# One of four transposing DMAs replaced by TensorE transposes, with a new hand-tuned task order

## The chip, the cores and the metric

The kernel runs on one core of one Trainium2 chip, as one launch. The metric is the device time of that launch in microseconds (us), lower is better. Each kernel was run several times. Names used below: PE is TensorE's matmul stream, DVE is VectorE, ACT is ScalarE, POOL is GpSimd, SP is the queue that issues hardware DMAs. "L512" is line 512 of the kernel's source.

## What is computed

Attention over 4 batches, 8 heads, 768 positions and 64 features per head. Heads 0, 2 and 6 see all earlier positions; heads 1, 3, 4, 5 and 7 see the last 64 positions and the first 4 ("sinks"). Its output, laid out as 3072 tokens by 512 features, goes through a gated feed-forward block. Shortened:

```python
scores = q @ k.T / 8, masked by head;  a = softmax(scores)
x = (a @ v) laid out as [3072, 512]
h = gelu(x @ w_gate) * (x @ w_val)              # 512 -> 1536
out = x + sigmoid(x @ w_res) * (h @ w_out)      # 1536 -> 512
```

## The kernel before

**Tiles and chunks.** The 3072 tokens are cut into six chunks of 512 tokens (`CHUNKS`; counted from 0, so the third chunk is chunk 2). Each chunk runs through the same stages. Attention comes first: for each of four head pairs, scores by TensorE into PSUM (L889, and L980 for the sinks), the exponential on ACT (L905), masks on DVE (L941), then the weighted sum of values on TensorE (L1013 for windows, and a helper at L512 and L513 for the rest), and the normalisation on DVE (L1078, L1080). Then come the matmuls with `w_gate` and `w_val` (called g and v, 96 per chunk and four per output block), gelu on ACT (L1162), and the product on DVE (L1164). Last come the outputs: `w_res` with a tanh (L1222), and seven products that make four output tiles of a pair from Strassen-like sums (L1253, L1277, L1282), and the write to memory from SP (L1288, and L1323 for the first pair of chunk 0).

**From tokens to features.** g and v need the normalised attention output with features on the partitions. The normalised values of a chunk are kept as 16-bit numbers in a buffer `x16` with two feature blocks of 128 at a time; two head pairs fill it, and it is then transposed into `xT`. Two ways stand in the source. `to_features` (L1100) makes four TensorE transposes of 128 by 128 per feature block (L1102) into a PSUM bank and one copy out of it by ACT or DVE (L1110). `to_features_dma` (L1092) makes one transposing DMA on SP (L1093) for both blocks. In chunks 0 and 1 all blocks go by TensorE. From chunk 2 (`DT_FIRST = 2`) the head pairs run in the order `LATER = (1, 3, 0, 2)`; the pairs 1 and 3, heads 4 to 7, fill feature blocks 2 and 3 first, and those go by DMA; blocks 0 and 1 follow by TensorE. The g and v matmuls over blocks 0 and 1 are tasks of their own and can run before blocks 2 and 3 are there.

**Loads.** POOL issues the loads that convert to 16 bits (L573). q and k of chunks 0 and 1 are transposed by TensorE (L705). From chunk 2 on SP issues eight transposing DMAs per chunk (L750) into `qkt`, and after a chunk's eight a copy of one head pair to other partitions, `q6` (L758); some of pair 1's score matmuls read `q6`. SP also issues the shifted copies of the values (L658). Each engine and each queue takes its instructions strictly in order.

**Who sets the order.** Every step is a task with an engine, an estimated cost, dependencies and a priority. A list scheduler written into the kernel (`Graph.schedule`) plays the tasks through with these estimates, and always starts the ready task of least priority number on each free engine; steps that two engines can do are given to the one that it expects to end first. The result is written out as fixed programs. Priorities follow a formula by chunk, and `HINTS` replaces single ones by numbers found beforehand; it lists them as task number and priority. Before the first g matmul the scheduler fills TensorE's idle time with matmuls on a blank tile (L1329). TensorE's instructions have four shapes: full 128 by 128, 64 rows (scores), 64 columns (windows, and from chunk 4 on nearly everything: L513 makes two 64-column matmuls of one) and 32 columns (sinks).

Of the kernel before, what the change touches and what calls it, by code (L numbers as in the profile page):

```python
# [39 lines left out]
DT_FIRST = 2  # L40
# [3 lines left out]


HINTS = (
    "1:-386.23 2:-51 9:-20.36 13:-200.31 428:1584.78 430:2007.77 436:2368.39 479:1475.25 482:1765.54 488:3518.86 "
    "537:6004.49 590:-192.92 609:-256.97 629:-1503.05 631:-966.95 638:-550.03 640:1715 643:232.16 648:262.35 "
    "656:219.8 674:810.58 675:-1134.51 703:38.07 711:336.34 712:-434.62 737:822.34 738:826.12 744:1130.99 "
    "750:1939.31 762:2550.75 767:1830.91 784:2410.9 787:-692.73 789:834.8 798:450.11 800:1192.39 805:3841.63 "  # L50
    "820:3905.53 831:1160.84 836:1677.33 837:940.96 841:627.82 848:508.5 865:-2323.53 877:2285.32 887:4400.62 "
    "898:3238.78 899:2548.8 906:2576.13 912:2498.5 918:2936.84 924:1499.5 955:3175.78 966:-173.61 967:2046.76 "
    "995:1370.62 1002:3719.58 1046:-2213.54 1051:2730.57 1053:3518.36 1060:4609.91 1063:5481.78 1087:3849.56 "
    "1119:6736.31 1120:3930.26 1131:2217.51 1137:3231.1 1138:3413.04 1143:2240.9 1150:3031.82 1156:5375.26 "
    "1168:2688.73 1187:2924.17 1196:2995.04 1216:2986.66 1243:1919.94 1247:2487.19 1252:5888.14 ~1253:3022.82 "
    "1257:2882.45 1260:4488.19 1309:6553.9 1315:4359.05 1326:4428.99 1367:1389.25 1372:1438.57 1374:3076.99 "
    "1387:1535.74 1388:5404.31 1391:3284.75 1451:6195.97 1454:3725.08 1457:4058.45 1459:6087.7 1478:5553.53 "
    "1481:6338.68 1482:6987.75 1495:6022.19 1510:6238.59 1511:4500.43 1513:5525.29 1520:4702.46 1525:4688.12 "
    "1530:4497.68 1538:4518.95 1544:4765.44 1547:2063.36 1549:4494.08 1562:6734.76 1567:1912.78 1568:5555.5 "
    "1577:4575.28 1591:4650.14 1594:5639.66 1596:9005.87 1614:9375.82 1619:4948.93 1622:4608.22 1654:6049.7 "  # L60
    "1659:4821.79 1673:5059.01 1674:6102.86 1678:6739.11 1688:4250.3 1689:6738.61 1691:14432.3 1744:5230.02 "
    "1800:10962.76 1802:6852.52 1803:7158.99 1804:6852.02 1805:7238.81 1811:7250.63 1817:6501.37 1818:5640.4 "
    "1820:10984.41 1835:7399.5 1836:6974.76 1839:7253.61 1840:7168.5 1842:7201.48 1843:7310.06 "
)

class Task:
# [42 lines left out]
class Pool:  # L109
# [7 lines left out]
    def can(self, kind, t):  # L117
        if kind in self.caps:
            h = self.held.get(kind, [])
            h[:] = [f for f in h if f is None or f > t]  # L120
            if len(h) >= self.caps[kind]:
                return False
        return any(f <= t for f, _ in self.free)
# [346 lines left out]
def build_kernel(nc, q, k, v, w_gate, w_val, w_out, w_res, out):  # L470
# [129 lines left out]
    def batch(b):  # L600
        if b not in batches:
            B_ = B()
            B_.v, B_.vs, B_.vk, B_.qkt = Buf(P_v), Buf(P_vs), Buf(P_vk), Buf(P_qkt)
            B_.vtok, B_.vstok, B_.qtok, B_.ktok = {}, {}, {}, {}

            B_.q6, B_.q6tok = None, {}
            batches[b] = B_
        return batches[b]
# [158 lines left out]
    def ph(c, part):  # L767
        return phase.setdefault((c, part), [])

    def attention(c, segs, xbuf, xtbuf, xtoks, xttoks, l0=0, last=(), ek=None, shared=None):  # L770
        tiles = [(b, i) for (b, a, z) in segs for i in range(a, z)]

        base = 1000 * c - (200 if len(tiles) < 4 and not l0 else 0)
        n0 = len(ph(c, "sc"))
        todo = []
        order = ORDER if c < DT_FIRST else LATER
        for k_, p in enumerate(order):
            P = B()
            P.heads, P.p, P.c, P.pr = PAIRS[p], p, c, base + 40 * k_
            retr = [IS_RETRIEVAL[h] for h in P.heads]  # L780


            banks, lower = [], []
            for x in range(2):
                mine = [[(b, i if retr[x] else None, i, 1) for b, i in tiles]]
                rest = [(b, kt, max(a, kt + 1), z - max(a, kt + 1)) for b, a, z in segs for kt in range(z - 1)] if retr[x] else []
                for r in sorted(rest, key=lambda r: -r[3]):
                    for bk in mine:
                        if sum(y[3] for y in bk) + r[3] <= 4:
                            bk.append(r)  # L790
                            break
                    else:
                        mine.append([r])
                if p == 1 and x == 1:

                    can = lambda bk: all((0, i) in batch(b).q6tok and (1, kt) in batch(b).q6tok
                                         for b, kt, q0, nq in bk for i in range(q0, q0 + nq))
                    left, mine = sorted(mine[1:], key=lambda bk: -sum(y[3] for y in bk)), mine[:1]
                    low = [bk for bk in left if can(bk)]
                    up = [bk for bk in left if not can(bk)]  # L800
                    while up or low:
                        mine.append((up or low).pop(0))
                        if low or up:
                            lower.append(id(low[0])) if low else None
                            mine.append((low or up).pop(0))
                banks += [(g, x, bk) for g, bk in enumerate(mine)]
            size = lambda t: sum(y[3] for y in t[2])
            if p != 1:
                banks.sort(key=lambda t: (t[0], -size(t), t[1]))
            else:  # L810
                banks.sort(key=lambda t: (t[0], -size(t) if not t[0] else 0, t[1]))
            P.et, P.off = (shared or {}).get(p, (None, 0))
            if P.et is None:
                P.et = Buf((P_eb if p else P_ea) if any(retr) else P_es)
            P.where, P.ready = {}, {}
            for g in range(0, len(banks), 2):
                scores(P, tiles, [t[1:] + (id(t[2]) in lower,) for t in banks[g:g + 2]], g, retr)
            if shared is not None and any(retr):
                shared[p] = P.et, P.off
            todo.append(P)  # L820
        sinks = sink_scores(c, [t for t in tiles if t[1] > 0], base + 40 + 5, ek, 256 if l0 else 0)
        for t in ph(c, "sc")[n0:-1]:
            if t.name[2:] in (str(order[2]), str(order[3])):
                t.order.append(ph(c, "sc")[-1])

        sc = ph(c, "sc")[:-1]
        for t, u in zip(sc[0::2], sc[1::2]) if c else ():
            t.deps += u.deps
            u.order.append(t)
            for b in u.bufs[:1]:  # L830
                t.bufs.append(b)
                b.left += 1
                b.users.append(t)
        norms = []
        for P in todo:
            if P.heads[0] % 2 == 0:
                x16 = Buf(P_x16)
                xdeps = []
            last, tn = weigh(P, tiles, sinks, xbuf, x16, xtoks, xdeps, last, l0)
            if P.heads[0] % 2 == 1:  # L840
                if c >= DT_FIRST and P.p == order[1]:
                    to_features_dma(c, P.heads[0] // 2, P.pr, x16, xdeps, xtbuf, xttoks)
                else:
                  for cb in (P.heads[0] // 2, P.heads[1] // 2):
                    to_features(c, cb, P.pr, x16, xdeps, xtbuf, xttoks, l0, len(tiles))
                if P is todo[-1]:
                    tn.order += [t for _, t in xttoks[-2:]]
                if c == 0 and P is todo[-1]:
                    for t in norms[1:]:
                        t.order.append(xdeps[-1])  # L850
            norms.append(tn)
        return last
# [239 lines left out]
    def to_features_dma(c, cb, pr, x16, xdeps, xtbuf, xttoks):  # L1092
        t = G.add("sp", 1.3, lambda e: e.dma_start(  # L1093
            at(xtbuf)[:, cb:cb + 2, :].rearrange("p c (i k) -> p (c i) k", k=128), at(x16)[:, :, :, :].rearrange("p c i k -> p (c i k)"), transpose=True),
            xdeps, pr - 4003, bufs=[x16, xtbuf], dma=1.2, name="xD")
        t.late = 2.5 if c == 2 else 1.0
        ph(c, "xT").append(t)
        xttoks += [(cb, t), (cb + 1, t)]
# [342 lines left out]
```

## Time and profile before

| | |
|---|---|
| median of 5 runs | 267.15 us (266.10, 266.24, 267.15, 268.81, 269.13) |
| profiled execution, its own time | 267.77 us |
| its span, first to last instruction | 266.0 us |
| granted TensorE clock | 1.00 |

Busy time in five stretches of the profiled execution, us:

| stretch | what runs | PE | DVE | ACT | POOL |
|---|---|---|---|---|---|
| 0 to 20 | loads, attention of chunk 0 | 16.00 of 20 | 10.32 | 10.29 | 17.20 |
| 45 to 67 | outputs of chunk 0, attention of chunk 1 | 22.00 of 22 | 19.05 | 15.84 | 8.65 |
| 67 to 88 | g and v of chunk 1 | 21.00 of 21 | 13.16 | 7.71 | 15.73 |
| 88 to 108 | outputs of chunk 1, attention of chunk 2 | 20.00 of 20 | 16.90 | 16.88 | 8.07 |
| 258 to 266 | last adds and writes | 3.73 of 8 | 5.35 | 0.60 | 2.29 |

An engine's busy time is what its instructions cover; PE's includes the blank matmuls. In the chain of waits, each piece is a start, a length, an engine and a line, with a count of instructions; a piece ends where the next thing that the end had to wait for begins. "To landing" is the time from a DMA's issue until its data has arrived.

### The profile page before, as it was taken

To read this page: it belongs to the slowest core of one execution; us is meant where nothing else is said; L and a number is where in the kernel's file an instruction comes from. 1 tells how busy PE (TensorE), PEld (TensorE's weight loads), DVE (VectorE), ACT (ScalarE), POOL (GpSimd) and SP (SyncE) were. 2 spreads that over 40 slices of the span, in tenths; PEclk is the share of its full clock that TensorE was granted. 3 is DMA by queue.
4 is the path that set the end of the run, shared out by engine and by line. 5 is a ranking of instruction groups with operands and counts; after the bars stand their busy time and mean duration, and the time that the engine had idled before them with its cause. 6 is when DMAs were issued, how large, how long until landed. Compare 5 with 4: busy or idle time off the path is not lost.

```text
span 266.0 us, 7506 instructions
## 1 busy us (share of the span) xinstructions
PE 257.4 (97%) x3234; PEld 166.6 (63%) x3234; DVE 181.8 (68%) x384; ACT 145.0 (55%) x229; POOL 89.7 (34%) x127
## 2 busy tenths in 40 slices
PE   7699999999999999999999999999999999999993
PEld 6567665457544577544477544679655589766792
DVE  2489536789656688664878645888448678936656
ACT  2576349875143889233786333787334887233430
POOL 8979979611995080994000000000000000000003
PEclk9999999999999999999999999999999999999999
DMA  6999999999999999999999300013110003110013
GB/s 83 160 205 206 187 175 229 176 152 170 129 152 237 172 130 144 190 157 184 183 154 147 126 0 0 2 43 84 39 43 0 2 2 82 58 65 0 2 38 123
DMA packets 97569, 29.49 MB, mean 111 GB/s; under 512 B 85504, under 2 KB 94080, under 8 KB 97536
## 3 DMA queue, kind: packets, MB, share of 16 engines
q0 software_dynamic: 70320, 14.69, 69.6%
q1 hardware_dynamic: 27216, 14.33, 29.9%
q8 instruction: 25, 0.41, 0.6%
q14 instruction: 8, 0.07, 0.1%
HBM read 29.36 MB, written 6.29 MB: 134 GB/s over the span
## 4 chain that ended last, share of the span: by engine, by line
PE 91%; DVE 4%; DMA 3%; POOL 1%; issue 0%; POOLq 0%
PE ps L512 48%; PE ps L513 32%; PE ps L889 5%; DMA qks<-in_k_dram 3%; PE ps L1013 2%; PE ps L1102 1%; PE ps L705 1%; DVE otile L1277 1%; POOL qks L573 1%; PE ps L1329 1%; PE ps L980 1%; DVE vs L642 1%; DVE otile L1253 1%; DVE otile L1282 0%; DVE x L1078 0%
## 5 line engine op out<-in xcount | busy, mean ns | idle before, releaser
L1162 ACT ACTIVATE gact<-ps 128x512 f16<-128x512 f32 x68 | 40.4, 597 | 72.5 <-PE ps L512 44.6
L1164 DVE SCALAR_TENSOR_TENSOR hT<-gact,ps 128x512 f16<-128x512 f16 x68 | 45.5, 686 | 46.9 <-ACT gact L1162 18.7
L512 PE MATMUL ps<-xT,wg 128*128 128x512 f16 (+1 forms) x208 | 50.6, 363 | 0.0
L512 PE MATMUL ps<-xT,wv 128*128 128x512 f16 (+1 forms) x202 | 50.2, 362 | 0.0
L1282 POOL TENSOR_TENSOR otile<-otile,xtok 128x256 f32<-128x256 f32 x3 | 2.3, 764 | 137.6 <-DVE otile L1277 137.6
L512 PEld LDWEIGHTS ps<-xT,wg 128*128 128x128 f16 x208 | 20.0, 98 | 20.9 <-DVE hT L1164 0.2
L573 POOL DMA_DIRECT2D qks<-in_k_dram x36 | 28.2, 815 | 13.1 <-DMA qkt<-qks 9.8
L512 PEld LDWEIGHTS ps<-xT,wv 128*128 128x128 f16 x202 | 19.4, 98 | 18.7 <-issue 0.3
L513 PE MATMUL ps<-xT,wv 128*64 128x512 f16 x204 | 29.4, 379 | 0.0
L573 POOL DMA_DIRECT2D qks<-in_q_dram x36 | 28.4, 828 | 2.4 <-issue 1.6
L573 POOL DMA_DIRECT2D va<-in_v_dram x24 | 21.3, 929 | 18.1 <-PE ps L512 18.1
L513 PE MATMUL ps<-xT,wg 128*64 128x512 f16 x192 | 27.2, 379 | 0.0
L905 ACT ACTIVATE ea<-ps 128x1024 f16<-128x1024 f32 (+2 forms) x24 | 21.1, 915 | 2.2 <-PE ps L889 1.9
L1253 DVE TENSOR_TENSOR otile<-otile,ps 128x256 f32<-128x256 f32 x33 | 13.6, 415 | 7.7 <-PE ps L512 3.1
L513 PEld LDWEIGHTS ps<-xT,wv 128*64 128x64 f16 x204 | 12.8, 110 | 8.9 <-ACT gact L1162 0.4
L1222 ACT ACTIVATE srs<-ps 128x512 f32<-128x512 f32 x22 | 13.1, 597 | 8.7 <-PE ps L513 5.9
L513 PEld LDWEIGHTS ps<-xT,wg 128*64 128x64 f16 x192 | 12.3, 110 | 7.9 <-DVE hT L1164 0.2
L1080 DVE TENSOR_TENSOR xtok<-ps,rcp 128x512 f32<-128x512 f32 (+1 forms) x28 | 16.7, 608 | 0.1
L889 PE MATMUL ps<-qkt 64*128 64x64 f16 (+4 forms) x391 | 16.3, 213 | 0.4 <-DVE xT L1110 0.4
L513 PE MATMUL ps<-wr,xT 128*64 128x512 f16 x120 | 15.3, 380 | 0.0
L889 PEld LDWEIGHTS ps<-qkt 64*128 64x128 f16 x391 | 9.7, 94 | 8.0 <-issue 4.0
L512 PE MATMUL ps<-wo,hT 128*128 128x256 f16 (+1 forms) x84 | 14.2, 303 | 0.0
(109 smaller groups left out, 437.1 us busy)
## 6 DMA issues: line engine op xcount, KB each, us to landing
out_dram<-otile SPq DMA_DIRECT2D x22, 256.0 KB, 3.2
va<-in_v_dram POOLq DMA_DIRECT2D x24, 128.0 KB, 13.4
qks<-in_k_dram POOLq DMA_DIRECT2D x32, 64.0 KB, 16.7
qks<-in_q_dram POOLq DMA_DIRECT2D x32, 64.0 KB, 16.5
wg<-in_moe_w_gate_dram POOLq DMA_DIRECT2D x3, 512.0 KB, 12.8
wv<-in_moe_w_val_dram POOLq DMA_DIRECT2D x3, 512.0 KB, 14.6
wo<-in_moe_w_out_dram POOLq DMA_DIRECT2D x4, 384.0 KB, 23.0
vs<-va SPq DMA_DIRECT2D x4, 260.0 KB, 8.4
```

The source lines that it names most:

```text
L512: return e.matmul(o, lhsT=lhsT, rhs=rhs, **k)
L513: return [e.matmul(o[h:h + 64], lhsT=lhsT[:, h:h + 64], rhs=rhs, **k) for h in (0, 64)][-1]
L573: return G.add(eng, issue, lambda e: e.dma_start(out_ap(), in_ap), deps, prio, bufs=bufs, dma=cost, name=name, grp=grp)
L642: return e.activation(out=o, in_=i_, func=AF.Copy) if on == "act" else e.tensor_copy(out=o, in_=i_)
L889: return [e.matmul(at(scr)[:, oo:oo + w], lhsT=side(BB, low, 1)[half, k0:k0 + 128], rhs=side(BB, low, 0)[half, qq:qq + w], start=True, sto ...
L905: return e.activation(out=o, in_=i_, func=AF.Exp, scale=SM_SCALE)
L1013: r.append(e.matmul(at(av)[64 * s:64 * s + 64, o:o + 65], lhsT=at(P.et)[:, w + 64 * s:w + 64 * s + 64], rhs=val, start=lt == 0 and (n == 4 ...
L1080: t2 = G.add("dve", c_dve(2 * n * 64), lambda e: e.tensor_tensor(out=xview(), in0=avv(0, DHEAD), in1=scale(), op=ALU.mult), [t1] + xdeps, ...
L1162: ta = G.add("act", c_act(512), (lambda gb=gb, ga=ga: lambda e: e.activation(out=at(ga)[:, :], in_=at(gb)[:, :], func=AF.Gelu))(), [tg], p ...
L1164: th = G.add("dve", c_dve(512), (lambda vb=vb, ga=ga, f=f: lambda e: e.scalar_tensor_tensor(out=hv(f), in0=at(ga)[:, :], scalar=0.5, in1=a ...
L1222: tas.append(G.add("act", c_act(512), (lambda rb=rb, sr=sr: lambda e: e.activation(out=at(sr)[:, :], in_=at(rb)[:, :], func=AF.Tanh, scale ...
L1253: return G.add("dve", c_dve(256), lambda e: e.tensor_tensor(out=dst(), in0=dst(), in1=at(D)[:, 0:256], op=ALU.add), [t, k], pr, bufs=[D, o ...
```

## The change

The test for the transposing DMA is made strict, so that it applies from chunk 3 on, and `HINTS` is replaced as a whole (142 entries before, 171 after, both cut here). Chunk 2's part has one DMA task less and four tasks more (two times four transposes, two copies out), so task numbers behind it stand for other tasks than before.

```diff
 HINTS = (
-    "1:-386.23 2:-51 9:-20.36 13:-200.31 428:1584.78 430:2007.77 436:2368.39 479:1475.25 482:1765.54 488:3518.86 "
...
-    "1820:10984.41 1835:7399.5 1836:6974.76 1839:7253.61 1840:7168.5 1842:7201.48 1843:7310.06 "
+    "3:-58.9 11:-130.04 428:854.14 430:718.61 444:2782.08 457:-821.9 460:407.45 490:4205.68 521:1522.06 "
...
+    "1834:7419.08 1836:10250.4 1849:7490.55 "
 )
...
             if P.heads[0] % 2 == 1:
-                if c >= DT_FIRST and P.p == order[1]:
+                if c > DT_FIRST and P.p == order[1]:
                     to_features_dma(c, P.heads[0] // 2, P.pr, x16, xdeps, xtbuf, xttoks)
                 else:
                   for cb in (P.heads[0] // 2, P.heads[1] // 2):
                     to_features(c, cb, P.pr, x16, xdeps, xtbuf, xttoks, l0, len(tiles))
```

In the written-out programs this gives eight TensorE transposes more (88 in place of 80) and four blank matmuls fewer (124 in place of 128), three transposing DMAs to `xT` in place of four, and two copies to `xT` more, one on ACT and one on DVE among those of 512 columns. Twelve full matmuls with `w_res` stand where 24 half ones did. The order differs on all five engines, in chunk 0 as well. On POOL, a memset and the select that makes the identity matrix now stand ahead of the second pair of q and k loads, where they stood behind it. On SP, two output writes of chunk 0 now stand behind the second of chunk 2's eight transposing DMAs and the other two behind the fifth; before, all four stood behind the eighth. Its copy `q6` then follows four transposing DMAs of chunk 3, where it followed two.

## The prediction

> **What bounds the kernel now.** I read the page first, then TensorE's own waits, then the chain of waits in order of time, and last the queue that the change touches.
>
> The page, shares and slices of the span:
>
> ```profile
> PE 257.4 (97%) x3234; PEld 166.6 (63%) x3234; DVE 181.8 (68%) x384; ACT 145.0 (55%) x229; POOL 89.7 (34%) x127
> ...
> PE   7699999999999999999999999999999999999993
> ...
> PE 91%; DVE 4%; DMA 3%; POOL 1%; issue 0%; POOLq 0%
> ```
>
> TensorE is full in every slice but the first two and the last, and carries 91% of the chain. A busy stream could still hide waits, so the next view asks what TensorE ever waited for (us in total, times, longest):
>
> ```profile
> PE ps L1329 <- DVE blank L545: 1.1, 1, 1.1
> PE ps L705 <- DMA qks<-in_q_dram: 1.0, 1, 1.0
> PE ps L705 <- DMA qks<-in_k_dram: 1.0, 1, 1.0
> PE ps L705 <- POOL ident L531: 0.8, 1, 0.8
> PE ps L889 <- DVE xT L1110: 0.4, 1, 0.4
> ```
>
> That is all, and all of it lies before 21 us. From there on TensorE's order is run without a gap. The chain (start, length, line, count) says what its pieces cost:
>
> ```profile
> 3.68 8.45 DMA qks<-in_k_dram
> ...
> 60.85 0.25 PE ps L1013 x8
> ...
> 64.79 0.38 PE ps L1013 x16
> ...
> 67.42 20.30 PE ps L512 x100
> ...
> 107.10 0.45 PE ps L1102 x8
> ...
> 186.40 20.30 PE ps L513 x200
> ```
>
> Three prices follow. A full matmul of g and v takes about 0.2 us (100 in 20.30), and so do two half ones (200 in 20.30). Eight transposes take 0.45 us. Eight window matmuls take 0.25 and sixteen 0.38, so eight more cost 0.13, and about 0.12 us is the fixed price of entering another shape. The kernel is TensorE's list plus a start (the first g matmul begins at 22.7 us in the timeline) plus a tail of about 5 us behind the last matmul. So an edit pays only if it shortens that list, the start or the tail, and costs only if it lengthens them or opens a gap.
>
> **The change, part by part.**
>
> *The DMA that goes.* The instructions that write xT by DMA, and who waited for them:
>
> ```profile
> L1093 SPq DMA_TRANSPOSE xT<-x x4: 1231/1254/3667, 100.6 to 222.3; - x4
> ...
>   PEld ps L512: 0.2, 1
> DMA to landing us min/median/max: 3.1/3.1/8.9
> ```
>
> The worst of the four, 8.9 us, is chunk 2's, issued at 100.6 and landed at 109.6. TensorE spent that time on outputs and on g and v over blocks 0 and 1, and a weight load waited 0.2 us for it, of which the matmul behind it lost about 0.1. So removing this DMA gives 0.1 us at most: it was hidden. SP is free of an issue of 3.67 us, behind which writes and loads for chunk 3 stood; nobody waited for those.
>
> The Trainium skill speaks against the removal: "Advanced Engine Details and Errata", section "X-Bar Transpose (TRN2)", holds transposing DMAs on this chip to be as fast as regular ones. Here the write issued next, at 104.35, landed 5.7 us later against 8.9, so the row is slower than the rule; by the rule the gain would be nothing and the sum 0.1 higher.
>
> *The transposes that come.* Eight full ones on a TensorE with no gap, by the row at 107.10: +0.45 us, all on the path. The two copies behind them cost ACT 0.60 and DVE 0.42 us (L1110, 128 by 512). In the stretch from 88 to 108 us those engines are busy 16.9 of 20 us each, so there is room; I take zero. If they were late, g and v would lack blocks 2 and 3 as they now lack blocks 0 and 1: at most 1.0 us, both copies on the path one after the other. Below zero it can't go.
>
> A second page prices the transposes higher: "VectorE: DVE Perf Modes", section "The three transpose paths", gives 390 ns for a 128 by 128 transpose on TensorE. Eight would be an estimated 3.1 us, and the whole sum 3.4; the trace's 0.056 us each, in a stream, decides against it.
>
> *The order on TensorE.* I counted the stretches of one shape in both written-out programs: 113 before and 115 after, from the first g matmul on 78 and 79. One more at 0.12: +0.1 us. Half matmuls against full ones (the `w_res` group) cost the same by the two 20.30 rows: zero.
>
> *The start.* On POOL a memset (L549, 0.25 us) and the identity select (L531, 0.32) move ahead of the second pair of q and k loads. The chain's first large piece is the last of these loads, 8.45 us to landing, so a later issue by up to 0.57 us can go straight into the end. For a gain speak the identity, for which the first transposes waited 0.8, and four fewer blank matmuls (0.06 each, 0.2). But q lands at 5.6 (issued at 1.3, 4.3 to landing), so the first transposes, at 6.0, can come forward by 0.3 at most, and k's, which follow, need a load that lands at 6.9 in either order. Bounds: -0.5 to +0.6. The loads already share the DMA engines with the first value loads, now issued earlier, which is nearer to the loss: I take +0.2.
>
> *The tail.* The last sixty matmuls and the last writes stand alike; DVE's last adds swap neighbours. Zero, bounded by one add of 0.42 us either way.
>
> Sum: -0.1 + 0.45 + 0.1 + 0.2 = about +0.7 us. Against the profiled execution's 267.77 that is 268.5. That execution lies 0.6 above the median of 267.15, so for the median I say 267.9.
>
> **The rivals.**
>
> *Rival 1, slower: chunk 2's `q6` comes after TensorE wants it.* The SP queue now (start, length to the last issue, count):
>
> ```profile
> 59.34 9.14 SPq L750 DMA_TRANSPOSE qkt<-qks  x6
> ...
> 78.20 0.60 SPq L1288 DMA_DIRECT2D out_dram<-otile  x1
> 79.11 0.67 SPq L758 DMA_DIRECT2D q<-qkt  x1
> ```
>
> Before, chunk 2's eighth transposing DMA is issued at 67.2 (9.6 to landing) and `q6` at 79.1 (7.4 to landing), so it is there at 86.5; TensorE first reads it at 90.7. In the new order SP stops, after two of the eight, at an output write that waits for the second add of chunk 0's first output pair (DVE L1319, ending 65.2 before; I take 65.5). Three DMAs at 1.33 each (9.14 over six, with waits in it) bring it to 69.5. Two more writes wait for chunk 0's last adds. The products before them now all stand ahead of chunk 1's g and v, ending at about 67.7 when I add up TensorE's rows, and DVE has some 3.5 us of work behind: 71.5. The last three DMAs go out by 75, the last landing at 83.5 with 8.4 to landing (the one at 75.5 took that), then four of chunk 3 until 81, and `q6` at 83.5, there at 91. TensorE's new order reads it later too, behind one more score group (0.54) and twelve products (1.42): 90.7 + 2.0 + 0.6 of the sum so far = 93.3. The margin falls from 4.2 to about 2.3 us. The landings of this stretch spread from 7.4 to 9.6, two of them in a row here, and my write time is uncertain by 1 us, so the margin can be used up. Each us beyond 93.3 is a us at the end, since TensorE is in order and everything is queued behind that score group. Priced at landing 2.5 us too late: 267.9 + 2.5 = 270.4. The same six DMAs release staging buffers for POOL's loads (it waited 9.8 us for such landings), so chunk 3's loads start some 5 us later; its own DMAs landed by 104 and are first read at 128, which covers that.
>
> *Rival 2, faster: the new order shortens the start.* Identity and blank matmuls give their 0.5, and chunk 0's reordered chain of ACT and DVE, the only place where TensorE runs blanks, gives as much again: 267.15 + 0.55 - 1.0 = 266.7; with the tail's 0.4, 266.3. Against it: the second k load, landing at 12.13, holds the chain in both. More than 1% would need 2.7 us, and by the prices above TensorE's list gets longer.
>
> *Rival 3: nothing.* The transfer was hidden and the start takes in the rest: 267.15. That the change does not do what it says is excluded by the counts in both programs.
>
> **How the numbers follow.** One per cent, about what a measurement here can tell from no change, is 2.7 us: the five runs of before spread over 3 us. Forecast case, a loss of 0.3 to 1.6: 60%. Rival 3: 8%. Rival 2: 12%, of which 3 beyond 1%. Rival 1, with any other new gap: 20%, nearly all beyond 1%. Faster 0.03, same 0.76, slower 0.21. The forecast's own range is 267.4 to 268.8. The range for 8 in 10 takes in most of rivals 1 and 2, the tail and the copies: 266.3 to 270.8.
>
> **What would show it.** Right: transposes (L1102) at 88 with 0.45 us more on the chain; TensorE's waits still nothing behind 21 us; three DMAs at L1093; the first g matmul within 0.6 of 22.7. Rival 1: a wait of L889 for `q` near 93 us. Wrong altogether: waits of g and v on ACT or DVE, or a start that moves by more than 1 us.

## The result, and the profile after

The changed kernel takes 265.92 us (median of 54 runs, 265.23 to 267.32) against 266.77 us before (94 runs, 265.56 to 270.32): ratio 0.9959, with a 95% interval of 0.9946 to 0.9972. Ratios leave out executions more than 1.5% above the fastest of their kernel, and they need not equal the quotient of the medians, which is 0.9968 here. The change is 0.4% faster, where a loss of 0.3% was forecast, and below the low end of the range. Its profiled execution took 265.94 us with a span of 264.1.

The page, with TensorE's share, its slices and the chain by engine:

```profile
PE 258.5 (98%) x3226; PEld 164.3 (62%) x3226; DVE 182.2 (69%) x378; ACT 147.2 (56%) x237; POOL 89.5 (34%) x127
...
PE   8999999999999999999999999999999999999993
...
PE 92%; DMA 3%; POOL 2%; DVE 1%; issue 0%; POOLq 0%
```

What TensorE waited for (us in total, times, longest):

```profile
PE ps L1333 <- DVE blank L549: 1.1, 1, 1.1
PE ps L516 <- DMA va<-in_v_dram: 0.2, 1, 0.2
PE ps L709 <- DMA qks<-in_q_dram: 0.2, 1, 0.2
```

Line numbers are four higher than before. TensorE's list is busier than before (258.5 against 257.4 us), yet the end comes earlier. Two waits of 1.0 us for q and k, one of 0.8 for the identity and one of 0.4 are gone, and a first slice of 7 has become 8. The chain starts with another load:

```profile
6.73 6.72 DMA va<-in_v_dram
20.02 1.54 PE ps L516 x16
```

Where a piece of 8.45 us for the fourth q/k load stood, there is now one for a value load. The first g matmul starts at 20.03 us (22.67 before). From there to the last matmul's end it is 239.97 us (239.07 before), and behind that 4.1 us (4.3). So the profiled pair differs by -2.64 + 0.90 - 0.15 = -1.9 us of span. Of that the medians show 0.85, since the execution of before that was profiled was itself 1.0 us above its kernel's median, and that of after was at its median.

The start on POOL in order of time, before and then after (start, length, line, operation):

```profile
1.31 0.91 POOL L573 DMA_DIRECT2D qks<-in_q_dram  x1 [0.80 <-POOLq L1423]
2.21 0.75 POOL L573 DMA_DIRECT2D qks<-in_k_dram  x1
2.95 0.76 POOL L573 DMA_DIRECT2D qks<-in_q_dram  x1
3.68 0.77 POOL L573 DMA_DIRECT2D qks<-in_k_dram  x1
```

```profile
2.22 0.75 POOL L577 DMA_DIRECT2D qks<-in_k_dram  x1
2.96 0.22 POOL L553 MEMSET m_causal<- 128x128 f16 x1
3.19 0.30 POOL L535 TENSOR_SCALAR_AFFINE_SELECT ident<-ident 128x128 f16<-128x128 f16 x1
3.43 0.77 POOL L577 DMA_DIRECT2D qks<-in_q_dram  x1
4.20 0.75 POOL L577 DMA_DIRECT2D qks<-in_k_dram  x1
```

The second pair is issued half a microsecond later, as the prediction says, but its q lands at 8.55 us instead of 10.72 and its k at 9.96 instead of 12.13. The two stretches in which its data moves, before and then after (PE, PEld, DVE, ACT, POOL busy, granted clock, DMA share, GB/s at the end):

```profile
6.40:9.40 3.00, 3.00 (x71) 2.43 (x66) 1.38 (x2) 1.97 (x4) 2.99 (x5) 1.00 1.29 157
```

```profile
6.40:9.40 3.00, 3.00 (x67) 2.52 (x66) 1.35 (x2) 1.69 (x4) 2.98 (x6) 1.00 1.47 188
```

From 4.0 to 6.4 us both kernels move 194 GB/s. Then before falls to 157, and after holds 188. By an estimate, that alone would make the fourth load 0.5 us late (31 GB/s less for 3 us is 93 KB). Why it is 2.2 us late can be seen in the sizes of the packets, the pieces in which a DMA moves its data. From 4.0 to 6.4 us, when only q and k move, 931 packets carry 0.47 MB and 20 of them are under 512 bytes: a q/k packet has 512 bytes. Many smaller ones come from 9.0 us on, with the value loads, which POOL issues next. From 9.5 to 12.1 us, before and then after:

```profile
DMA packets 2817, 0.41 MB, mean 157 GB/s; under 512 B 2678, under 2 KB 2817, under 8 KB 2817
```

```profile
DMA packets 3097, 0.41 MB, mean 157 GB/s; under 512 B 3094, under 2 KB 3096, under 8 KB 3096
```

So in the kernel before 139 of the 2048 packets of the two pairs (four loads of 256 KB) are still under way after 9.5 us, among the packets of the value loads, and the last of them sets the landing. After, 3 packets of this size or larger are left.

### The profile page after: what moved, and what is told of

It reads as the page before. It is cut to its first block, busy times and chain, and to the rows that moved or that the text cites. A ratio compares the mean times of both kernels' runs of the same rounds, so it can differ in the third digit from the quotient of the medians.

```text
span 264.1 us, 7495 instructions
## 1 busy us (share of the span) xinstructions
PE 258.5 (98%) x3226; PEld 164.3 (62%) x3226; DVE 182.2 (69%) x378; ACT 147.2 (56%) x237; POOL 89.5 (34%) x127
## 4 chain that ended last, share of the span: by engine, by line
PE 92%; DMA 3%; POOL 2%; DVE 1%; issue 0%; POOLq 0%
PE ps L516 50%; PE ps L517 32%; PE ps L893 5%; DMA va<-in_v_dram 3%; PE ps L1017 2%; PE ps L1106 2%; POOL qks L577 1%; PE ps L984 1%; PE ps L1333 1%; PE ps L709 1%; DVE otile L1281 1%; DVE otile L1286 1%; POOL va L577 0%; DVE otile L1257 0%; POOL m_win L535 0%
## 5 line engine op out<-in xcount | busy, mean ns | idle before, releaser
L1168 DVE SCALAR_TENSOR_TENSOR hT<-gact,ps 128x512 f16<-128x512 f16 x68 | 46.1, 686 | 48.0 <-PE ps L516 23.1
L516 PE MATMUL ps<-xT,wg 128*128 128x512 f16 (+1 forms) x208 | 50.0, 363 | 0.0
L516 PE MATMUL ps<-xT,wv 128*128 128x512 f16 (+1 forms) x202 | 49.0, 362 | 0.0
L517 PE MATMUL ps<-xT,wv 128*64 128x512 f16 x204 | 28.3, 380 | 0.0
L517 PE MATMUL ps<-xT,wg 128*64 128x512 f16 x192 | 26.3, 379 | 0.0
L517 PEld LDWEIGHTS ps<-xT,wv 128*64 128x64 f16 x204 | 11.4, 110 | 9.9 <-DVE hT L1168 0.3
L517 PEld LDWEIGHTS ps<-xT,wg 128*64 128x64 f16 x192 | 11.0, 110 | 9.1
L1286 DVE TENSOR_TENSOR otile<-otile,xtok 128x512 f32<-128x512 f32 (+1 forms) x21 | 14.3, 692 | 0.2
```

The source lines that it names most:

```text
L516: return e.matmul(o, lhsT=lhsT, rhs=rhs, **k)
L517: return [e.matmul(o[h:h + 64], lhsT=lhsT[:, h:h + 64], rhs=rhs, **k) for h in (0, 64)][-1]
L1168: th = G.add("dve", c_dve(512), (lambda vb=vb, ga=ga, f=f: lambda e: e.scalar_tensor_tensor(out=hv(f), in0=at(ga)[:, :], scalar=0.5, in1=a ...
L1286: fn = (lambda ot=ot, lt=lt, w=w: lambda e: e.tensor_tensor(out=at(ot)[:, w], in0=at(ot)[:, w], in1=at(xbuf)[:, lt, w], op=ALU.add))()
```

## The experiments

Two questions: does the new order of POOL's start bring this, or chance, or the new order of the tasks behind it; and what is the headline edit, eight transposes for one DMA, worth by itself. In most runs the priorities were played through as they are, and then the written-out list was edited, so that every other step keeps its place. The start runs replace POOL's first nineteen steps:

```diff
     span = G.schedule()
+    first = [390, 391, 3, 2, 392, 393, 4, 5, 394, 6, 395, 7, 396, 8, 397, 9, 379, 10, 380]
+    pool = G.prog["pool"]
+    G.prog["pool"] = sorted(pool, key=lambda t: first.index(t.seq) if t.seq in first else len(first) + t.pos)
```

390 to 393 are the four q/k loads, 394 to 397 the value loads, 2 the identity select, 3 and 4 the causal mask, 5 to 10 the window mask, 379 and 380 the first weights. The list above is that of the changed kernel (e1, e15). The others:

```diff
-before  390, 391, 392, 393, 3, 5, 4, 6, 2, 7, 394, 8, 395, 396, 397, 9, 379, 10, 380
+e2      390, 391, 392, 393, 3, 5, 4, 6, 2, 7, 394, 8, 395, 396, 397, 9, 379, 10, 380
+e3      390, 391, 3, 2, 392, 393, 5, 4, 6, 7, 394, 8, 395, 396, 397, 9, 379, 10, 380
+e4      390, 391, 392, 393, 3, 2, 4, 5, 394, 6, 395, 7, 396, 8, 397, 9, 379, 10, 380
+e12     390, 391, 3, 5, 4, 392, 393, 6, 2, 7, 394, 8, 395, 396, 397, 9, 379, 10, 380
+e13     390, 391, 3, 392, 393, 2, 5, 4, 6, 7, 394, 8, 395, 396, 397, 9, 379, 10, 380
+e14     390, 3, 2, 391, 392, 393, 5, 4, 6, 7, 394, 8, 395, 396, 397, 9, 379, 10, 380
```

All that was measured, in one table. "Pair 2" is when q and k of the second pair landed, "g" the first g matmul and "body" the time from there to the last matmul's end, all in us of the one profiled execution; the ratio is to the kernel before on the same chip, with its 95% interval. Medians of different chips and hours can't be compared closely: that of the kernel before was 266.19 to 267.31 beside these runs.

| run | pair 2 landed | g | body | median (lowest to highest) | ratio |
|---|---|---|---|---|---|
| before | 10.72, 12.13 | 22.67 | 239.07 | 266.77 (265.56 to 270.32) | |
| e11 before again | 10.04, 11.36 | 21.53 | 239.17 | 266.93 (265.96 to 268.54) | 1.0002 (0.9965 to 1.0039) |
| e2 after, old start | 9.85, 11.24 | 20.99 | 240.07 | 266.89 (265.90 to 269.53) | 1.0034 (1.0004 to 1.0065) |
| e4 values apart | 9.33, 11.01 | 21.12 | 239.39 | 266.23 (265.65 to 267.92) | 1.0000 (0.9975 to 1.0025) |
| e9 transposes alone | 11.16, 12.56 | 23.76 | 239.78 | 266.96 (266.40 to 269.53) | 1.0007 (0.9976 to 1.0039) |
| e13 short pause | 10.15, 11.54 | 21.88 | 239.45 | 266.82 (265.89 to 269.04) | 1.0005 (0.9964 to 1.0045) |
| e14 pause inside pair 1 | 9.33, 10.70 | 20.93 | 239.27 | 266.21 (265.92 to 267.89) | 0.9993 (0.9960 to 1.0026) |
| e12 pause, no identity | 8.38, 9.98 | 20.61 | 239.34 | 265.92 (265.05 to 267.83) | 0.9976 (0.9936 to 1.0016) |
| e3 pairs apart | 8.53, 9.87 | 19.93 | 239.00 | 266.09 (264.96 to 268.11) | 1.0011 (0.9982 to 1.0041) |
| e1 before, new start | 8.54, 9.88 | | | 265.84 (264.72 to 266.26) | 0.9991 (0.9976 to 1.0006) |
| e15 the same again | 8.62, 10.01 | 20.07 | 241.11 | 265.72 (264.75 to 267.20) | 0.9969 (0.9935 to 1.0002) |
| e10 pairs apart, transposes | 8.47, 9.83 | 19.80 | 239.77 | 266.56 (265.62 to 267.93) | 0.9978 (0.9947 to 1.0009) |
| after | 8.55, 9.96 | 20.03 | 239.97 | 265.92 (265.23 to 267.32) | 0.9959 (0.9946 to 0.9972) |
| e5 after again | 8.44, 9.79 | 19.85 | 239.77 | 266.00 (265.15 to 266.75) | 0.9966 (0.9940 to 0.9992) |
| e7 transposes twice | 8.61, 10.01 | 19.68 | 240.00 | 266.36 (265.63 to 266.91) | 0.9968 (0.9940 to 0.9996) |
| e6 after, DMA kept | 8.73, 10.12 | 20.26 | 245.52 | 270.47 (267.05 to 273.45) | 1.0108 (1.0066 to 1.0149) |
| e8 new hints | 8.64, 10.02 | 20.81 | 241.23 | 269.07 (267.99 to 275.51) | 1.0080 (1.0045 to 1.0115) |

In the profiled execution of e1 every matmul took about twice its time (525.45 us); it is left out of the median, and only its landings are used.

### The start

> The kernel before, with nothing changed but the order of POOL's first nineteen steps, which is that of the changed kernel (memset and identity select between the two q/k load pairs, a select between any two value loads). Start theory: the gain sits in this order and everything behind the first g matmul costs 0.5 to 0.6 us more in the changed kernel, so this one should be the fastest so far: about 265.3 us, first g matmul near 20 us, and a spread as narrow as that of the changed kernel (2 us). Rival, the body's new order makes the gain: 266.8, as before, first g matmul near 22.5. Rival, chance (the second pair's late landing comes and goes from execution to execution whatever the order): median near 266.8 and times spread from 265.6 to 270 as before.

> The changed kernel with POOL's first nineteen steps in the order of the kernel before. Start theory: the gain goes and the price of the transposes stays, so about 267.3 us (266.8 + 0.5), with single times up to 270. Rival, the body makes the gain: 265.9, no change against the changed kernel. Rival, chance: 265.9 with a narrow or a wide spread alike.

> The kernel before with only the memset and the identity select moved between the two pairs of q/k loads; the value loads stay behind the selects, three of them back to back. If the pause between the pairs is what lets the second pair land early: about 265.3 us as in the run with the whole new order, second pair landed by 10 us. If it is the selects between the value loads: 266.8 us and second pair landing at 10.7 and 12.1 in some executions. My theory of the prediction (a later issue lands later): second pair at 11.2 and 12.7, 267.3.

> The kernel before with the two pairs of q/k loads back to back as they are, but the identity select right behind them and a select between any two value loads as in the changed kernel. If the value loads, issued without a pause, hold the second pair up: about 265.3 us. If the pause between the pairs decides: 266.8 us, with single times up to 270 and the second pair landing as late as 12 us. The identity alone, 0.8 us earlier at the first transposes, can give at most 0.3 us of this.

The order decides when the second pair lands. Back to back (before, e2, e4, e9, e11) its k comes at 11.0 to 12.6 us in five of five executions, whatever the body; with the memset and the identity between the pairs (after, e1, e3, e5, e6, e7, e8, e10, e15) at 9.8 to 10.1 in nine of nine. By the packets of 512 bytes or more from 9.5 to 12.1 us it is the same division: 69 to 139 in the five, 1 to 13 in the nine. Selects between the value loads (e4) are not the cause, and the prediction's theory, 11.2 and 12.7 us in e3, falls. With the pairs apart TensorE's waits in e3 are down to the first one, which every kernel has:

```profile
PE ps L1329 <- DVE blank L545: 1.1, 1, 1.1
```

In e2 TensorE waits for the second pair and the identity as in the kernel before:

```profile
PE ps L709 <- DMA qks<-in_k_dram: 0.9, 1, 0.9
PE ps L709 <- POOL ident L535: 0.8, 1, 0.8
```

In the times the gain is smaller than in the landings. With the old start the changed kernel loses its whole gain: 1.0034 (e2) against 0.9959 and 0.9966 (after, e5), intervals apart, and 0.9 us by medians from different chips. "The body makes the gain" falls: in e2 it stays behind by 0.3% with an interval above 1. That the new start alone makes the old kernel faster is not shown: e1 (0.35 us by medians, against 266.19 on its chip), e3, e12 and e15 have ratios of 0.9969 to 1.0011, and every interval takes in 1.

> The kernel before, unchanged, for a second look at its start. If back-to-back pairs are what lands late: q and k of the second pair at 9.3 to 10.7 and 11.0 to 12.1 us again, and a wait of TensorE for them; if chance: 8.5 and 9.9. And whether TensorE waits for chunk 2's transposing DMA in this execution.

> The kernel before with two memsets and the causal select between the q/k load pairs instead of behind them; the identity select stays behind the second pair. If POOL's pause of about half a microsecond between the pairs is what lets the second pair land early: 8.5 and 9.9 us, as in all eight executions with the pairs apart. If it is the identity (TensorE's first transposes earlier): 9.3 to 11.2 and 11.0 to 12.6, as in all five with the pairs together.

> The kernel before with only the memset of the causal mask (0.25 us on POOL) between the pairs. If the pause works by its length: in between, k of the second pair at 10.2 to 11.0 us. If any instruction between the pairs is enough: 9.9. If a quarter of a microsecond does nothing: 11.0 to 12.6.

> The kernel before with the memset and the identity select between q and k of the first pair, so that k and the second pair follow back to back. If what counts is that not four (nor three) loads are issued in a row: early, 9.9 us for the last. If the pause has to stand at the third load, when the first packets move (from 2.95 us on): late, 11 to 12.6 us, and first-pair k at 7.4 besides.

These three are one profiled execution each. Without the identity in the pause (e12, issue of the third load at 3.69 us) the pair lands as early. The first g matmul still starts at 20.61 us there, 0.5 to 0.8 later than with the old body and the identity in the pause (19.80 to 20.07 in e3, e10, e15), so the place of the identity, or of the masks that took it, may be worth that much. The memset alone moves the issue only from 2.95 to 3.09 us and does nothing (11.54), so it isn't a matter of any instruction between. Inside the first pair it does a part: 10.70, with the first pair's k at 7.96 instead of 6.95. What works in full is a pause of about half a microsecond ahead of the third load, with the first two issued at once. Why is open: the runs don't tell what slows the queue between 6.4 and 9.4 us, nor why a part of the pair's packets falls behind.

> The kernel before with POOL's first nineteen steps in the new order, once more, for its profile and its times: the profiled execution of the first run had every matmul at twice its time. Start theory: second pair landed by 10 us, no wait of TensorE for q or k, first g matmul at 19.9 to 20.5, fastest execution near 264.7. Its median was 265.84 without that execution, 1.1 above its fastest: whatever holds the usual execution up should show as a wait behind the start, for the value loads, or at 104 us for the transposing DMA of chunk 2 (0.4 us and more).

What ran as e8 was another kernel than its expectation describes: the start entries of `HINTS` were exchanged and the scheduler played again, which reorders all engines from chunk 0 on.

```diff
 HINTS = (
-    "1:-386.23 2:-51 9:-20.36 13:-200.31 428:1584.78 430:2007.77 436:2368.39 479:1475.25 482:1765.54 488:3518.86 "
+    "3:-58.9 11:-130.04 428:1584.78 430:2007.77 436:2368.39 479:1475.25 482:1765.54 488:3518.86 537:6004.49 "
```

With the same good start it is 0.8% slower than before: TensorE waits on ACT and DVE in chunk 2, and the body is 241.23 us. Here the start hints cost more by the order that they upset than they give. e15 is the run that was meant:

> The kernel of the first run (the order before, POOL's first nineteen steps as in the changed kernel), once more for a usable profile and a second set of times. By what the runs have shown: second pair at 8.5 and 9.9 us, first g matmul at 19.9 to 20.2, no granted clock below 0.996, median 265.6 to 265.9, at or a little below the changed kernel (265.92 and 266.00), since it leaves out the 0.5 us of the edit.

Its median, 265.72, agrees with e1. But its profiled execution took 267.20, with a body some 2 us longer than that of e3, and the start is not why. TensorE's waits, and the chain at 99 us:

```profile
PE ps L512 <- DMA xT<-x: 1.4, 1, 1.4
```

```profile
97.00 1.62 PE ps L512 x10
99.52 9.66 DMA xT<-x
109.22 18.63 PE ps L512 x87
```

This is the transposing DMA that the change removes. Issued at 99.5 us, it landed 9.7 later, while in e3 (100.1) it needed 6.8 and nobody waited. With the start 2.6 us earlier, TensorE wants blocks 2 and 3 earlier too, and a DMA that was just hidden is no longer hidden in this execution (1.4 us of the 2; in e13, with its first g matmul at 21.88 us, TensorE waited 0.2 for it).

### The edit by itself

> The changed kernel as it is, beside the next three on one chip, and a second look at its start. If the order of the start decides and not chance, the second pair of q/k loads lands at 8.5 and 9.9 us again (10.7 and 12.1 in the kernel before), the first g matmul is near 20 us and the time 265.9, within 265.2 to 267.3.

> The changed kernel with only its headline edit undone: blocks 2 and 3 of chunk 2 go by the transposing DMA again, and their eight transposes and two copies are taken out of the written-out programs; every other step keeps its place. My step of the prediction (the DMA is hidden but for 0.1 us, the eight transposes cost 0.45 on TensorE): 0.35 us faster than the changed kernel, 265.5, so the edit itself is a loss. Rival: the earlier start and the longer SP queue leave the DMA too little time, it lands behind the last g or v matmul over blocks 0 and 1, and TensorE waits 0.4 us or more for it: as the changed kernel or slower, 265.9 to 266.5, and the edit is no loss.

> The changed kernel with the eight new transposes issued twice into the same place. If they stand on the path at 0.056 us each: 0.45 us more than the changed kernel, 266.35, and eight more instructions in the rows at 99 and 103 us with 0.45 us more TensorE time. If they fill a wait (for a bank, or for the copies of the products): less than 0.2 us more.

e6, in the written-out programs of the changed kernel:

```diff
 TensorE
-L1106 Matmult ps<-ident,x 128x128 x4
...
-L1106 Matmult ps<-ident,x 128x128 x12
+L1106 Matmult ps<-ident,x 128x128 x8
 DVE and ACT, one each
-L1114 xT<-ps 128x512
 SP
-L754 DmaTransposeAnt qkt<-qks 128x4x128 x3
+L754 DmaTransposeAnt qkt<-qks 128x4x128
+L1397 DmaTransposeAnt xT<-x 128x8x128
+L754 DmaTransposeAnt qkt<-qks 128x4x128 x2
```

It is about 4 us slower than the changed kernel (4.5 by the medians, 3.8 by the ratios 1.0108 and 0.9966). The DMA (all at one tile; the first numbers are the length of its issue in ns, least, median and most, then its start), and TensorE's wait for it:

```profile
L1397 SPq DMA_TRANSPOSE xT<-x x1: 4031/4031/4031, 101.8 to 101.8; - x1
```

```profile
PE ps L516 <- DMA xT<-x: 4.6, 1, 4.6
```

In the new order TensorE wants blocks 2 and 3 at 106.8 us, and the DMA, 4.0 us in its issue and 9.6 to landing, brings them at 111.4. Its data was complete at 100.9 us (DVE L1082) and it was issued at 101.8, so an earlier place on SP could have saved 0.9 us and not the whole wait. In the profiled execution the body is 5.75 us longer than in e5: 4.6 of wait and, by an estimate, 1.7 of the clock that falls to half behind it for 3.4 us, less the transposes. The rival of that expectation holds, at more than ten times its least price of 0.4: in this order, which was tuned without this DMA, the edit is worth about 4 us, not a loss of 0.35.

For e7, which leaves the result as it is, the list of transposes reads

```diff
-            for i in range(n) for h, w in (((0, 64), (64, 64)) if G.run == "col" else ((0, 128),))],
+            for _ in range(2 if c == 2 and cb > 1 else 1) for i in range(n) for h, w in (((0, 64), (64, 64)) if G.run == "col" else ((0, 128),))],
```

The chain around them in the changed kernel and in e7:

```profile
101.63 0.22 PE ps L1106 x4
...
104.87 0.67 PE ps L1106 x12
105.54 0.11 PE ps L516
105.65 0.04 issue
```

```profile
101.09 0.45 PE ps L1106 x8
...
104.55 0.89 PE ps L1106 x16
105.45 1.74 PE ps L516 x14
```

0.056 us each, on the path: four more in 0.22, twice. The median rose by 0.36 (266.36 against 266.00 on the same chip), a little less than 0.45. A short stall behind the last transposes, of which the "issue" piece is a part, closed at the same time: between the starts of the next two matmuls there are 0.32 us in the changed kernel and 0.11 in e7. The scatter of single times (1.3 to 1.6 us) is larger than this difference, so the price rests on the chain.

> The kernel before with the headline edit alone: chunk 2's transposing DMA to xT is out, its eight transposes stand in one place (two free PSUM banks, behind the weighted sums of pair 2), the two copies on ACT and DVE; every other step keeps its place, the start too. By the sum of the prediction: 0.45 to 0.6 us slower than before, 267.3 by the median of this day, spread up to 270 as before. Rival, from the run with the DMA kept (TensorE waited 4.6 us for it): in part of the executions of the kernel before TensorE waits for this DMA too, and the single times above 268 with a granted clock of 0.984 to 0.993 are those. Then they vanish: no time above 268, median 266.3 or less, although the fastest is 0.4 slower (266.0).

> The same, and the memset and the identity select between the two q/k load pairs, as in the run with the pairs apart. If start and DMA are two separate gains: the narrowest of all, fastest near 265.4, median 265.5 to 265.9, nothing above 267. If the start alone matters: as the run with the pairs apart plus 0.45, 266.5, up to 268.5. If the DMA alone: as the run before this one.

Both put the eight transposes into the kernel before, in one place and with nothing else moved (e10 with e3's start besides):

```diff
 TensorE
 L512 Matmult ps<-va,ea 128x65 x18
+L1394 Matmult ps<-ident,x 128x128 x8
 L512 Matmult ps<-wt,hS 128x256 x6
 DVE
 L941 TensorTensor es<-es,m_win 128x1024
+L1397 TensorCopy xT<-ps 128x512
 ACT
 L905 Activation es<-ps 128x1024
+L1397 Activation xT<-ps 128x512
 SP
-L1093 DmaTransposeAnt xT<-x 128x8x128
```

The body rises from 239.0 to 239.5 (before, e3, e4, e11 to e14) to 239.78 and 239.77: 0.3 to 0.8 us, of which the profile shows 0.45 for the transposes and 0.2 of waiting for an ACT copy (L1248) that the new copy pushed back. The fastest executions rise by the same: 266.40 against 265.57 in e9, 265.62 against 264.96 in e10. The other rival falls: e9's times still reach 269.5, so the long times don't need the DMA. e9's profiled execution, 269.53 us, shows one source of them (columns as above), first e9 and then the kernel before:

```profile
9.00:13.00 4.00, 2.02 (x47) 1.44 (x43) 1.12 (x2) 2.22 (x3) 4.00 (x8) 1.00 2.24 160
13.00:14.00 1.00, 1.00 (x19) 0.68 (x18) 0.94 (x4) 0.43 (x1) 0.43 (x2) 0.80 1.63 195
14.00:17.00 3.00, 3.00 (x42) 2.08 (x38) 2.31 (x6) 2.15 (x5) 2.88 (x7) 0.50 1.28 205
17.00:20.00 3.00, 3.00 (x62) 2.12 (x60) 2.19 (x9) 1.94 (x6) 3.00 (x4) 1.00 1.25 207
```

```profile
9.00:13.00 4.00, 1.96 (x37) 1.40 (x35) 1.49 (x3) 1.84 (x3) 4.00 (x8) 1.00 2.11 158
...
14.00:17.00 3.00, 3.00 (x65) 2.09 (x63) 2.14 (x8) 2.63 (x7) 2.12 (x5) 1.00 1.34 203
```

In both, the late pair leaves TensorE busy for 2 of the 4 us from 9 to 13. In e9 its granted clock then falls to 0.50 until 17 us, and it does 42 matmuls there instead of 65: about 3.4 us at half speed, 1.7 us lost. In the other execution it stays at 1.00. So the late pair cost its wait in every profile, and the clock besides in this one. By the mean granted clock of each run, 28 of 133 executions of the kernel before, timed beside these runs, were below 0.995, and none of 145 of the kernels with a pause of half a microsecond and no long wait later (after, e1, e3, e5, e7, e10, e12, e14, e15). With a late pair there were 2 of 12 in e2, 2 of 10 in e13, 1 of 12 in e9 and none of 12 in e4. That the clock fell at the start in those 28 was not seen. Of the 41 of the 133 that took more than 267.5 us, 13 had a clock of 0.996 or more; what lengthened them is open.

## Why the prediction was wrong

**The start, the step that failed.** The prediction takes +0.2 within bounds of -0.5 to +0.6, because "a later issue by up to 0.57 us can go straight into the end". It read 8.45 us to landing as a latency that moves with its issue, where a part of the load's packets had fallen behind. The rows of before could have told: the first pair's q and k landed 1.30 us apart, so at the rate of the first two the fourth would have landed at 5.63 + 3 x 1.30 = 9.5 us. It landed at 12.13, and those 2.6 us were excess that an order of issues could take away. With the pause the fourth lands at 9.8 to 10.1. In the profiled pair the start term was -2.64 us; against the second look at the kernel before (e11) it is -1.5. The prediction's other reason for a loss, the value loads issued earlier, shows no cost: e1 and e15 issue the first at 5.45 us, e3 and e10 at 6.32, and the pair lands alike.

**The prediction's rival 2** had the right sign and was dismissed for the same reason: "the second k load, landing at 12.13, holds the chain in both". Its own sources, the identity and the blanks, are not what let the pair land early, since it does so without the identity in the pause (e12); of the start they may be worth the 0.5 to 0.8 us by which e12's first g matmul is later.

**The eight transposes** cost 0.45 on the path, as said (e7, and 0.22 per four in the chain). The copies, taken as zero within 1.0, cost about 0.2 in e9 and e10; in the changed kernel, too, a short stall stands behind the transposes. With the other stretches of the new order the body costs 0.3 to 1.0 us (239.77 and 239.97 against 239.0 to 239.5) where the sum had 0.45 without the start.

**The DMA that goes** was put at 0.1 because its wait was 0.2 on a weight load. For the order and the start of before that is right. It is no property of the DMA: with the early start TensorE waited 1.4 us for it in e15, and in the new order 4.6 (e6). The early start alone gives the lowest single times of all (264.72 and 264.75); the changed kernel's lowest is 265.15. What the transposes buy is that nothing hangs on this DMA. Of the old body with a pause (e1, e3, e12, e15) 4 of 45 times lie above 267.5, of the changed kernel's 66 (with e5) none. That the DMA is behind those four is not shown: e15's wait of 1.4 us gave 267.20, and e10, which has no such DMA, has one time of 267.93 in 12.

**Rival 1** did not come about. In the trace `q6` of chunk 2 was issued at 81.1 us, landed at 88.8 and was first read at 90.3. The margin was 1.5 us where 2.3 had been estimated, and no wait arose. **Rival 3** falls with the interval below 1. Of the signs named, the transposes, the three DMAs and the absence of waits behind 21 us held; "a start that moves by more than 1 us" was the sign for wrong, and it came.

**A version better than both** could be the old body with the new start (e15), which leaves out the price of the transposes. Its median (265.72) and ratio (0.9969, up to 1.0002) can't be told from the changed kernel's.

## What to carry to other kernels

Set a load's time to landing against the spacing of its neighbours of the same size: what exceeds it may be a stall that another order of issues removes, as it was here, so "issued later" need not mean "there later". A hidden transfer is hidden for one timing only; before it is priced at nothing, ask what it costs when everything ahead of it gets faster. And look at the spread of the times, not at one profile: the kernel before, whose times reach 1.8% above its fastest, has something in it that its one profile did not show.

## What was not expected of the hardware

- Four 256 KB loads issued by POOL without a pause move 157 to 172 GB/s in the stretch from 6.4 to 9.4 us (before, e2, e4, e9, e11), and 180 to 189 with a pause of half a microsecond ahead of the third (the nine with the identity in it, and e12). The last then lands at 9.8 to 10.1 us instead of 11.0 to 12.6, although it is issued 0.5 to 0.8 later. Without the pause 69 to 139 of their packets trail behind 9.5 us, among those of the value loads. The cause is open.
- TensorE's granted clock fell to 0.50 for 3.4 us after a stretch of 4 us in which it was half idle (e9, above), and after the 4.6 us wait of e6 (0.50 from 113 to 115 us). The Trainium skill, "TensorE: Matmul & The Clock Gate", section "Part 1: The HAM clock gate", states that an idle window of about 3.4 us halves the clock, that a busy one restores it, and that the window runs freely. The rows agree in the depth and the length, and e6 in the idle time. In e9 TensorE's longest wait in that stretch was 1.0 us, so an idle time of 3.4 us was not needed. The free-running window would be a reason why the same idle time cost nothing in the execution of before; no run here shows the window itself.
